# The first unit's decays by other operations, and the pieces of the first two units in one explicit list

## The chip, the cores and the metric

One core of one Trainium2 chip. The time is that of the device from launch to end, in microseconds (us), as the median of several executions. The span in a profile (first to last instruction) is 1.7 to 1.9 us shorter than the time of the same execution, in all executions but two of `tags_old` (2.3 and 2.4).

The five engines work at once, each through its own queue, in order: TensorE (PE, with its weight loads as PEld), VectorE (DVE), ScalarE (ACT), GpSimd (POOL) and SyncE (SP, which here only issues transfers). PSUM is the buffer that TensorE writes its results to. The clock in a profile is the granted clock, the share of TensorE's full clock that it was given in that stretch.

## The reference

A gated linear attention with complex decays, followed by an ELU layer with two weight matrices.

```python
# q, k, v, a_re, a_im: (4, 8, 768, 48) float32
mag   = sqrt(a_re**2 + a_im**2)
scale = minimum(mag, 0.999) / (mag + 1e-6)
for t in range(768):
    S = (a[t] * scale[t]) * S + outer(k[t], v[t])      # complex S, 48 x 48 per head
    y[t] = q[t] @ real(S)
x = y as (3072, 384)
h = x @ w_in                                           # w_in (384, 2048)
g = where(h > 0, h, exp(minimum(h, 0)) - 1)
return (g @ w_out).astype(float32)                     # w_out (2048, 384)
```

The two weight matrices arrive as float64. The kernel makes float32 of them with bit operations on VectorE.

## The kernel before

The work is cut into 12 units of 256 tokens (two batches, 128 positions). For every unit the kernel takes logarithms of the decays' lengths, angles, running sums of both over the positions (by matmuls with a triangular matrix), exponentials and sines; it scales q and k with them, transposes them on TensorE, makes scores, states and values, brings the result into the layer's layout by six small transfers (the "seam"), and then runs the layer: 8 pieces `hidden` (12 matmul instructions each, 2.6 us) and 8 groups `project` (8 instructions each, 2.6 to 2.8 us).

The weights come in 16 parts of 786 KB, 8 of each matrix. Each is converted in five VectorE instructions of 128 x 768, the last of which is the addition below:

```python
    def rounded(kind, m):
        w, dst = raw.pop((kind, m))
        ...
        yield from _rounded(nc, w, f, p)          # four bit operations
        nc.vector.tensor_tensor(out=dst, in0=p, in1=f, op=ALU.add)
        done.append((kind, m))
        yield True

    def converts(n):                              # the next n of these 80 instructions
        ...
```

What comes when is set by numbers. Every piece of work is put into a plan with a position; the plan is sorted, and the result is the order in which each engine's queue is filled:

```python
    decays_of(0, *map(us, (6, 8, 8, 13.4, 13, 13.2, 13.3, 13.5, 13.5)))
    ...
    layer_of(0, 4, 20)
    layer_of(1, 12, 28)
    ...
    for at in range(4, 24):
        put(at + 0.1, converts, 3)
    ...
    for u in range(2, NU):
        if u == 2:
            decays_of(u, 16, 17, 17, 18.4, 19.5, 19.6, 22.7, 19.8, 19.8)
            gates_of(u, 20.4, 21.6, 22.1, 22.4, 22.6)
    ...
    for _, _, do in sorted(plan, key=lambda x: x[:2]):
        do()
```

So in `before` unit 2's decays and gates (positions 16 to 22.6) stand between the conversions (positions up to 23.1) in VectorE's queue. Every unit also sends its decays at the ends of chunks (64 positions each) through a buffer in DRAM and back, to get them transposed.

Of the kernel before, what the change touches and what calls it, by code (L numbers as in the profile page):

```python
# [16 lines left out]
C = 128  # L17
L = 64
# [486 lines left out]
def kernel(  # L505
# [33 lines left out]
    def const(a, name):  # L539
        a = np.ascontiguousarray(a, dtype=np.float32)  # L540
        t = cst.tile(list(a.shape), FP32, name=name)
        nc.scalar.dma_start(out=t, in_=nc.inline_tensor(a, name=name + "_c").ap())
        return t
# [6 lines left out]
    i = np.arange(C)  # L550
    upto = i[:, None] <= i[None, :]
    own = i[:, None] // L == i[None, :] // L

# [4 lines left out]
    off = cst.tile([C, 4], FP32, name="off")  # L558
# [4 lines left out]
    def work(shape):  # L563
        return ps.tile(shape, FP32, tag="w", bufs=3, name="w")
# [40 lines left out]
    def weights_of(kind, m):  # L605

        if kind == "in":
            n = WF * DM // NI
            dst, cols = w_in[:, :, ts(m, n)], ts(m, 2 * n)
            t = sb.tile([C, WF * DM, 2], U32, tag="g" + str(int(m > 1)), bufs=2, name="w64")  # L610
# [72 lines left out]

    def squares(u):
        x = nat[u]
        ar, ai = x["ar"], x["ai"]
        x["m2"], sq = new("n", 6), new("n", 6)
        nc.scalar.activation(out=x["m2"], in_=ar, func=AF.Square)
        nc.scalar.activation(out=sq, in_=ai, func=AF.Square)  # L689
        products(u).tensor_tensor(out=x["m2"], in0=x["m2"], in1=sq, op=ALU.add)  # L690
        x["sq"] = sq

    def logarithms(u):


        x = nat[u]
        lm = x["m2"]
        x["w"], x["e"], x["t"] = new("n", 6), new("n", 6), new("n", 6)
        nc.scalar.activation(out=x["w"], in_=x["ar"], func=AF.Ln)
        nc.scalar.activation(out=lm, in_=lm, func=AF.Ln)  # L700

    def powers(u):
        x = nat[u]
        nc.scalar.activation(out=x["t"], in_=x["w"], func=AF.Exp, scale=-1.0)
        nc.scalar.activation(out=x["e"], in_=x["m2"], func=AF.Exp, scale=-0.5, bias=ln_eps)

    def ratios(u):
        x = nat[u]
        w, t = x["w"], x["t"]
        products(u).tensor_tensor(out=w, in0=x["ar"], in1=t, op=ALU.mult)  # L710
        products(u).tensor_tensor(out=t, in0=x["ai"], in1=t, op=ALU.mult)

    def lengths(u):
        x = nat[u]
        x["l"] = lm = x["m2"]
# [12 lines left out]
    def noted(u):  # L728
# [3 lines left out]
        if u < 2:  # L732
            sq = nat[u]["sq"]
            for n, (x, scale, bias) in enumerate(((sq, 1.0, most_sq), (ar, -1.0, least_re))):
                nc.scalar.activation(
                    out=sq, in_=x, func=AF.Relu, scale=scale, bias=bias,
                    accum_out=off[:, 2 * n + u : 2 * n + u + 1],
                )
            return
        nc.vector.tensor_reduce(  # L740
            out=least[:, u : u + 1], in_=flat(ar), axis=mybir.AxisListType.X, op=ALU.min
        )
        nc.vector.tensor_reduce(
            out=most[:, u : u + 1], in_=flat(ai), axis=mybir.AxisListType.X, op=ALU.max,
            apply_absolute_value=True,
        )
# [3 lines left out]
    def angles(u):  # L750
        x = nat[u]
        x["th"] = new("n", 6)
# [12 lines left out]
    def turns(u):  # L765
        x = nat[u]
        x["z"] = new("n", 6)
        for n in range(NB):
# [11 lines left out]
            )  # L780
        nxt = u + B // NB
        if nxt < NU:
            carry[nxt] = new("carry", 2, [1, NB * HD])
            nc.gpsimd.dma_start(out=carry[nxt], in_=flat(x["z"])[C - 1 : C])  # L784

    def decays(u):
# [3 lines left out]
        for n in range(NB):  # L790
            t = work([C, HD])
            nc.tensor.matmul(  # L792
                t, lhsT=sum_logs, rhs=x["l"][:, n].rearrange("p h d -> p (h d)"),
                start=True, stop=True,
            )
            for key, sign in (("E", 1.0), ("F", -1.0)):
# [3 lines left out]
                )  # L800
        ends = dram.tile([NB, C // L, H, D], FP32, tag="ends", bufs=2, name="ends")
# [6 lines left out]
    def waves(u):  # L808
        x = nat[u]
        x["cs"] = new("cs", 1, [C, NB * H, 2, D])  # L810
        z = x["z"].rearrange("p n h d -> p (n h) d")
        nc.scalar.activation(out=x["cs"][:, :, 1], in_=z, func=AF.Sin, scale=TURN)
        cos = x["cs"][:, :, 0]
        nc.scalar.activation(out=cos, in_=z, func=AF.Abs)
        nc.scalar.activation(out=cos, in_=cos, func=AF.Sin, scale=-TURN, bias=quarter)

    def scaled(u):
        x = nat[u]
        products(u).tensor_tensor(out=x["k"], in0=x["k"], in1=x["F"], op=ALU.mult)
        nc.vector.tensor_tensor(out=x["q"], in0=x["q"], in1=x["E"], op=ALU.mult)  # L820
# [6 lines left out]
    def gated(u):  # L827

        x = nat[u]
        o = {key: new(key + "g", 1, [C, NB, H, 2, D]) for key in ("k", "q")}  # L830
        step = NB if u > 1 else 1
        for n in range(0, NB, step):
            for key in ("q", "k") if u < 2 else ("k", "q"):
                eng = products(u) if key == "k" else nc.vector
                each = x[key][:, n : n + step].rearrange("p n h d -> p (n h) d")
                eng.tensor_tensor(  # L836
                    out=o[key][:, n : n + step].rearrange("p n h i d -> p (n h) i d"),
                    in0=each.unsqueeze(2).to_broadcast([C, step * H, 2, D]),
                    in1=x["cs"][:, n * H : (n + step) * H], op=ALU.mult,
                )  # L840
# [29 lines left out]
    def states(u, n):  # L870
# [8 lines left out]
        gs = [work([2 * D, H, D]) for c in range(last)]  # L879
# [49 lines left out]
    def seam(u):  # L929

        x = nat[u]
        for j in range(2):
            for i in range(NI):
                eng = nc.scalar if u < 2 and j else nc.gpsimd
                eng.dma_start(  # L935
# [4 lines left out]
    def hidden(u, f):  # L940
        x = nat[u]
# [3 lines left out]
        t = ps.tile([C, 2, GT], FP32, tag="mlp", bufs=3, name="mlp")  # L945
        for e in range(2):
            for i in range(NI):
# [3 lines left out]
                )  # L951
# [198 lines left out]
```

## Time and profile before

| | before |
|---|---|
| time, median of 3 | 768.64 us (766.08 to 769.48) |
| span and time of the profiled run | 763.8 and 765.6 us |
| TensorE busy, of the span | 718.8 us, 94% |
| last weight part converted | 158.5 us |
| first layer piece of unit 2 | 203.1 us |
| from there on, TensorE | full |

Two more lines from the view of waits, VectorE's waits from 0 to 160 us (who waited for what, the total in us, how often, the longest):

```profile
DVE wf L39 <- DMA w<-in_moe_w_in_dram: 11.1, 3, 6.4
...
DVE g L955 <- ACT ee L954: 8.8, 3, 5.2
```

VectorE is the bound of the start, and yet stands still 20 us of it in these two groups alone: because input weights were not there, and because it had come, in its own order, to the second half of a layer piece whose first half ScalarE had not finished.

### The profile page before, as it was taken

How to read it: one execution, taken by the hardware profiler on the slowest of the kernel's cores; microseconds unless marked ns; L12 is line 12 of the kernel's file. 1: busy time of each engine (PE TensorE's matmuls, PEld its weight loads, DVE VectorE, ACT ScalarE, POOL GpSimd, SP SyncE). 2: the span in 40 equal slices, each digit the busy share in tenths (PEclk: the TensorE clock that was granted, in tenths of full speed). 3: DMA queues.
4: the chain of work that ended last, by engine and by line, in shares of the span. 5: the costliest groups of instructions: out<-in, count | busy, mean ns of one | idle time of the engine just before them, and what ended most of it. 6: DMA issues, size and time to landing. Idle time of an engine off the chain costs nothing.

```text
span 763.8 us, 13152 instructions
## 1 busy us (share of the span) xinstructions
PE 718.8 (94%) x5502; PEld 537.6 (70%) x5502; DVE 305.6 (40%) x416; ACT 390.2 (51%) x597; POOL 196.7 (26%) x192
## 2 busy tenths in 40 slices
PE   6978787889999999999999999999999999999995
PEld 5756676456686686686786786786786786786773
DVE  3698579933322532532532432432432423320120
ACT  6755237336445646646546546546546546541220
POOL 0101000104614504504404404405405405402000
PEclk9879899899999999999999999999999999999999
DMA  9959716162320810810810810810800900100000
GB/s 175 161 99 188 124 49 186 42 104 46 65 64 1 163 51 2 160 54 2 169 44 3 172 41 7 169 40 12 167 36 14 168 33 18 52 1 17 10 1 26
DMA packets 143885, 56.09 MB, mean 73 GB/s; under 512 B 128920, under 2 KB 133576, under 8 KB 143816
## 3 DMA queue, kind: packets, MB, share of 16 engines
q1 hardware_dynamic: 139392, 53.49, 34.6%
q0 software_dynamic: 3584, 1.27, 1.6%
q8 instruction: 45, 0.74, 0.4%
q10 hardware_dynamic: 840, 0.40, 0.2%
q14 instruction: 24, 0.20, 0.1%
HBM read 49.14 MB, written 4.79 MB: 71 GB/s over the span
## 4 chain that ended last, share of the span: by engine, by line
PE 80%; DVE 6%; DMA 6%; ACT 3%; issue 2%; SPq 1%; POOL 1%; ACTq 0%; DVEq 0%; POOLq 0%
PE mlp L965 30%; PE mlp L948 30%; PE w L853 5%; PE w L882 4%; DMA w<-in_moe_w_in_dram 4%; PE w L861 3%; PE y L912 3%; PE w L792 2%; PE w L770 2%; PE y L905 2%; DMA w<-in_q_dram 1%; DVE wp L49 1%; DVE wf L42 1%; DMA ends<-n 1%; SPq L631 1%
## 5 line engine op out<-in xcount | busy, mean ns | idle before, releaser
L965 PE MATMUL mlp<-w_out,g 128*128 128x384 f32 x768 | 264.8, 494 | 0.2 <-DVE g L955 0.2
L948 PE MATMUL mlp<-x,w_in 128*128 128x256 f32 x1152 | 262.8, 383 | 0.7 <-DMA x<-y 0.7
L948 PEld LDWEIGHTS mlp<-x,w_in 128*128 128x128 f32 x1152 | 216.2, 191 | 33.0 <-ACT o L971 1.3
L965 PEld LDWEIGHTS mlp<-w_out,g 128*128 128x128 f32 x768 | 143.6, 192 | 93.5 <-issue 2.9
L955 DVE SCALAR_TENSOR_TENSOR g<-ee,mlp 128x512 f32<-128x512 f32 x96 | 65.9, 687 | 213.1 <-ACT ee L954 174.7
L953 ACT ACTIVATE ee<-mlp 128x512 f32<-128x512 f32 x96 | 57.2, 596 | 151.1 <-PE mlp L948 150.6
L895 POOL TENSOR_TENSOR S<-S,T 96x384 f32<-96x384 f32 x36 | 35.6, 989 | 218.6 <-DVE S L893 218.6
L954 ACT ACTIVATE ee<-ee 128x512 f32<-128x512 f32 x96 | 60.5, 630 | 2.9
L935 POOL DMA_DIRECT2D x<-y x66 | 32.5, 499 | 59.9 <-ACT y L924 59.8
L971 ACT COPY o<-mlp 128x384 f32<-128x384 f32 x24 | 11.5, 480 | 66.5 <-PE mlp L965 65.6
L893 DVE TENSOR_TENSOR S<-w,S 96x384 f32<-96x384 f32 x40 | 22.1, 552 | 55.3 <-PE w L882 38.1
L920 ACT COPY x<-y 128x384 f32<-128x384 f32 x24 | 11.5, 478 | 62.9 <-PE y L912 62.9
L882 PEld LDWEIGHTS w<-vn,kg 64*96 64x96 f32 x704 | 34.7, 161 | 9.7 <-issue 9.3
L784 POOL DMA_DIRECT2D carry<-n x10 | 5.1, 505 | 130.3 <-DVE n L778 109.7
L882 PE MATMUL w<-vn,kg 64*96 64x48 f32 x704 | 37.8, 247 | 0.0
L853 PE MATMUL w<-ident,qg 128*96 128x128 f32 x192 | 26.5, 284 | 11.9 <-DVE a L866 7.2
L690 POOL TENSOR_TENSOR n<-n 128x768 f32<-128x768 f32 x9 | 16.4, 1819 | 82.9 <-ACT n L689 82.9
L866 DVE TENSOR_TENSOR a<-w,mask 128x512 f32<-128x512 f32 x24 | 16.5, 688 | 51.7 <-PE w L861 51.7
L836 POOL TENSOR_TENSOR kg<-k,cs 128x1536 f32<-128x1536 f32 x9 | 34.1, 3789 | 10.1 <-issue 10.0
L853 PEld LDWEIGHTS w<-ident,qg 128*96 128x96 f32 x192 | 22.4, 131 | 16.0 <-DVE a L866 7.6
L854 ACT COPY qt<-w 96x512 f32<-96x512 f32 x48 | 25.4, 576 | 15.3 <-PE w L853 15.3
L792 PE MATMUL w<-n,sum_logs 128*128 128x384 f32 x48 | 21.8, 585 | 10.0 <-DVE n L716 10.0
(94 smaller groups left out, 784.0 us busy)
## 6 DMA issues: line engine op xcount, KB each, us to landing
w<-in_moe_w_out_dram SPq DMA_DIRECT2D x16, 768.0 KB
w<-in_moe_w_in_dram SPq DMA_DIRECT2D x8, 768.0 KB
w<-in_moe_w_in_dram SPq DMA_DIRECT2D x16, 288.0 KB
vn<-in_v_dram SPq DMA_DIRECT2D x24, 192.0 KB
out_dram<-o SPq DMA_DIRECT2D x24, 192.0 KB
ar<-in_a_re_dram SPq DMA_DIRECT2D x22, 192.0 KB
ai<-in_a_im_dram SPq DMA_DIRECT2D x22, 192.0 KB
q<-in_q_dram SPq DMA_DIRECT2D x22, 192.0 KB
```

Source lines behind the costliest of these rows:

```text
L792: nc.tensor.matmul(t, lhsT=sum_logs, rhs=x["l"][:, n].rearrange("p h d -> p (h d)"), start=True, stop=True,)
L836: eng.tensor_tensor(out=o[key][:, n : n + step].rearrange("p n h i d -> p (n h) i d"), in0=each.unsqueeze(2).to_broadcast([C, step * H, 2, ...
L853: nc.tensor.transpose(t[:, h], x[key + "g"][:, n, h0 + h], ident)
L854: nc.scalar.copy(out=o[:, h0 : h0 + 4], in_=t)
L882: nc.tensor.matmul(g[:, h], lhsT=x["kg"][ts(c, L), n, h], rhs=vn[u % 2][ts(c, L), n, h, 0:D], start=True, stop=True,)
L895: eng.tensor_tensor(out=new_s, in0=new_s, in1=wide, op=ALU.mult)
L935: eng.dma_start(out=x["x"][ds(j * HP + D, G), i], in_=x["y"][ds(j * HP + i * G, G)])
L948: nc.tensor.matmul(t[:, e], lhsT=w_in[:, i, ts(f + e, C)], rhs=x["x"][:, i], start=(i == 0), stop=(i == NI - 1),)
L953: nc.scalar.activation(out=e, in_=t, func=AF.Relu, scale=-1.0)
L954: nc.scalar.activation(out=e, in_=e, func=AF.Exp, scale=-1.0)
L955: nc.vector.scalar_tensor_tensor(out=x["g", f // 8][:, f % 8 : f % 8 + 2], in0=e, scalar=-1.0, in1=t, op0=ALU.add, op1=ALU.max)
L965: nc.tensor.matmul(x["o", n], lhsT=x["g", f // 8][:, f % 8, ts(n, C)], rhs=w_out[:, f], start=(f == 0), stop=(f == NF - 1),)
```

## The change

Two things at once. The first unit's decays use other operations: the squares are joined by TensorE in PSUM (an addition by two accumulating matmuls), VectorE's reciprocal gives the ratio of imaginary to real part, the sum of capped logarithms is split into two accumulating matmuls, and the chunk ends are picked by matmuls instead of a trip through DRAM (units 0 and 1). GpSimd makes the constant matrices instead of four transfers. And the order of the start is an explicit list, up to unit 2's layer; it interleaves the first layers of units 0 and 1 with their attention, moves unit 2's decays behind all conversions, and lets input parts 4 to 7 use the buffers `w64` that the output parts also use. The diff is cut to its main lines.

```diff
-    ident = const(np.eye(C), "ident")
-    sum_turns = const(upto / (2 * np.pi), "sum_turns")
+    ident = const(C, C, "ident")
+    nc.gpsimd.memset(ident, 0.0)
+    nc.gpsimd.affine_select(out=ident, in_=ident, ...)
...
+    def joined(u):                               # u == 0: squares added on TensorE
+        for key in ("m2", "sq"):
+            for n in range(NB):
+                nc.tensor.matmul(x["both"][n], lhsT=ident, rhs=flat(x[key][:, n : n + 1]),
+                    start=(key == "m2"), stop=(key == "sq"))
...
+    def inverses(n):
+        nc.vector.reciprocal(out=x["t"][:, n], in_=x["ar"][:, n])
...
+    def ends(u):                                 # u < 2: picked by matmuls
+                    nc.tensor.matmul(t[:, n, :, h], lhsT=x["E"][:, n, h],
+                        rhs=ident[:, L - 1 :: L], start=True, stop=True)
...
-            t = sb.tile([C, WF * DM, 2], U32, tag="g" + str(int(m > 1)), bufs=2, name="w64")
+            tag = "g" + str(m // 2) if m < 4 else "w64"
...
-    layer_of(0, 4, 20)
-    layer_of(1, 12, 28)
-    for at in range(4, 24):
-        put(at + 0.1, converts, 3)
+    first = [
+        (warm, 3), (warm, 9), (begun, 0), (squares, 0), (fetch, "in", 0), (load_v, 0),
+        ...
+        *3 * [(convert,)], (ends, 1), (inner, 0, 0), (ratios, 1), (scaled, 1), (noted, 1),
+        ...
+        (inner, 1, 12), (inner, 1, 14), (elu, 1, 12), (elu, 1, 14), *15 * [(convert,)],
+        (fetch, "out", 7), *24 * [(convert,)], (project, 1, 0, 0, 4), (project, 1, 0, 4, 8),
+        *10 * [(convert,)], (begun, 2), *5 * [(convert,)], (project, 0, 0, 0, 4),
+        ...
+        (project, 0, 0, 8, 12), (squares, 2), (joined, 2), (logarithms, 2), (noted, 2),
+        ...
+    ]
```

`inner` is the matmul half of a layer piece and `elu` its second half on ScalarE and VectorE.

## The prediction

> **What bounds the kernel now.** I read the page's busy rows and slices first, then the windows, the chain that ended last, and last the timeline of the first 205 us. All times are from the span's start.
>
> The page and its slices:
>
> ```profile
> PE 718.8 (94%) x5502; PEld 537.6 (70%) x5502; DVE 305.6 (40%) x416; ACT 390.2 (51%) x597; POOL 196.7 (26%) x192
> ...
> PE   6978787889999999999999999999999999999995
> ...
> DVE  3698579933322532532532432432432423320120
> ```
>
> A slice is 19 us. TensorE is busy 94% on average, but the loss is all in the first nine slices; there VectorE is the busy engine (9, 9 in slices 7 and 8). The 40% of VectorE is an average over two different kernels: a start and a steady stage. The windows say it with numbers (columns: sum of the stretch, then PE, PEld, DVE, ACT, POOL busy, clock, DMA, GB/s):
>
> ```profile
> 0.00:20.00 20.00, 12.57 (x83) 11.78 (x84) 8.45 (x10) 12.87 (x16) 0.89 (x10) 0.91 1.19 177
> 20.00:40.00 20.00, 18.54 (x231) 15.49 (x232) 13.54 (x20) 16.57 (x24) 2.52 (x3) 0.92 1.17 159
> 40.00:60.00 20.00, 14.99 (x135) 11.47 (x132) 18.44 (x26) 11.18 (x19) 2.79 (x5) 0.74 0.51 99
> ...
> 120.00:140.00 20.00, 15.50 (x49) 10.30 (x49) 18.60 (x25) 12.29 (x16) 0.00 (x0) 0.83 0.62 174
> 140.00:160.00 20.00, 14.14 (x44) 7.98 (x43) 17.63 (x21) 8.34 (x12) 2.64 (x3) 0.91 0.20 31
> ...
> 300.00:400.00 100.00, 100.00 (x750) 75.72 (x750) 36.95 (x50) 53.95 (x84) 36.65 (x34) 1.00 0.39 82
> ```
>
> From 300 us TensorE is never idle: nothing there can be won except by less matmul work, and the change takes none away. The chain says where the steady stage begins:
>
> ```profile
> 152.52 1.75 DVE kg L836
> 154.27 1.68 DVE qg L836
> 156.09 1.63 PE w L853 x8
> ...
> 203.12 8.10 PE mlp L948 x36
> ...
> 260.47 7.77 PE mlp L948 x36
> ```
>
> At 203.12 the first layer of unit 2 (the third of 12) starts; the next unit's starts at 260.47, then every 57.0 us. So the time is (start of that layer) + 560.7 us to the end of the span + 4.8 us between the span of 763.8 and the median of 768.64. I need one number: when the changed kernel reaches that layer. Before it, TensorE has to do two units of 57.0 us, the attention of unit 2 (57.0 less 96 x 0.216 and 64 x 0.322 for the layers = 15.7) and 2.9 of unit 3: 132.6 us. Some 70 of the 203 us are therefore idleness, cold clock and the dummy "warm" matmuls (10.8 + 6.9 + 2.7 = 20.4 us).
>
> What they wait for is weights. They arrive as float64 in 16 parts, each converted by five VectorE instructions:
>
> ```profile
> 50.98 0.56 DVE L39 TENSOR_SCALAR wf<-w 128x768 uint32<-128x768 uint32 x1
> 51.57 0.96 DVE L42 SCALAR_TENSOR_TENSOR wf<-w,wf 128x768 uint32<-128x768 uint32 x1
> 52.56 0.56 DVE L45 TENSOR_SCALAR wp<-wf 128x768 uint32<-128x768 uint32 x1
> 53.16 0.96 DVE L49 SCALAR_TENSOR_TENSOR wp<-w,wp 128x768 f32<-128x768 uint32 x1
> 54.15 0.96 DVE L642 TENSOR_TENSOR w_in<-wp,wf 128x768 f32<-128x768 f32 x1
> ```
>
> From 50.98 to 55.11 that is 4.13 us a part, 66 us for 16. The last part of the output weights is done at 158.5 us, behind unit 2's gates in VectorE's order. So until 158 us the bound is VectorE (118.8 busy of 160 us, summed over the windows) with holes: first data at 5.6 us, 11.1 us waiting for input weights (three waits, by the view of waits), and waits for ScalarE.
>
> **The Trainium skill.**
> "TensorE: Matmul & The Clock Gate", Part 1, says that an idle array falls to half clock and regains it after some 3.4 us of work. The trace agrees: the four matmul instructions of one decay sum took 2.93 us at 18.26 and 1.45 us at 185.39. I count early ones cold.
> "ScalarE: Activation LUTs", What ACT_TABLE_LOAD costs, gives 1283 ns for every switch of set; the trace has 1.28 us each time. The same page's table of sets has one with both exp and ln, but the kernel's loads show that exp after ln costs one here.
> "VectorE: DVE Perf Modes", in its walkthrough's hardware budget, says that reciprocal is an iterative divide with a repeat count of 8. No row of this trace has one. Estimates for 384 elements: 0.56 us if it runs like the trace's other 384-element operations, eight passes at the 0.96 GHz of the skill's opening page 3.2 us.
>
> **The change part by part.**
> (1) Constants made by GpSimd in place of four transfers, the log table loaded ahead of the data: saves the 1.28 us load that followed the data at 5.62, and 0.2 MB of traffic.
> (2) Unit 0's decays. Removed on VectorE: the join of squares 0.96, two ratios shrunk from 1.91 to 1.15, a length from 0.95 to 0.56, a slope 0.95. Added: two reduces 1.9, two reciprocals 1.1 to 6.4, four sign clears (both units) 2.2, small copies 0.6. VectorE ends 2.7 to 8 us of work heavier; the dearer reciprocal would mostly fill the hole from 7 to 12 us in which the first weights are still under way. ScalarE loses an Ln, an Exp and two noted passes with accumulator reads for unit 0 (about 3.9 us) and the Abs of both. Chain of unit 0 as I step it: squares 8.5, joined on TensorE and Ln by 12 (I allow one useless table load), Exp 14.3, sums 16.7, E and F 17.4, arctan 19.5, turns 22.9, gates from 26 to 29.7, against 27.6 to 31.1 before: 1.5 us gained. The picks of the chunk ends (32 matmul instructions by about 0.11, 3.5 us) replace a DRAM round trip of 4.33 + 2 us that ends in a 2.0 us wait of VectorE, but hold VectorE about as long before the scaling.
> (3) Order. First layers of unit 0 and 1 interleaved with attention: unit 0's layer may start near 44 us instead of 57.02. Unit 2's decays move behind all conversions: 15.2 us of VectorE work (0.95 + 3.8 + 0.95 + 2.2 + 1.9 + 3.5 + 1.9) leave the path to the last weight. Input parts 4 to 7 go through the two buffers of unit 1's inputs and then of the output weights, so 12 parts pass through two buffers.
> VectorE to the last conversion, by starts rather than durations: through unit 1's gates with four parts 50.1; part 4 with mask, states and layer 7.1; then 11 parts 45.6, 14 layer pieces at 0.62 8.7, the rest of unit 1's states 2.3. Sum 113.8.
> Holes: 5.5 before data; 4.5 for Ln and the first weights; 4 for the picks; 1.5 in unit 1. That puts the second half of the parts at about 73 us. A part is 786 KB: 4.2 us at the 177 to 188 GB/s of the page's full slices, plus about 2 us from issue to landing. With two buffers and 3.1 us until a buffer is free again, a pair takes about 6.4 + 4.1 = 10.5 us against 8.3 of VectorE; unit 2's inputs (2 MB, 10.5 us) lie in the same queue. Stepped part by part, holes of 6.6 more. Last conversion: 113.8 + 5.5 + 4.5 + 4 + 1.5 + 6.6 = 135.9, say 136 us against 158.5.
> TensorE from there: the last layer piece of unit 1 is at about 118; then 16 projection groups by 2.6 = 41.4 (10 of them need only weights that are there before 130) and 2.9 for unit 2's sums: 162. Unit 2's decays, started at 136, are gated at about 162 too. Then there is no projection left to hide the attention of unit 2: transposes, copies, scores, states on GpSimd (0.82 each), values, six GpSimd issues by 0.5 and 1.6 us landing. I step 23 us for 11.5 of matmuls: 185.
> 185 against 203.1: 18 us earlier. 768.6 - 18 = 750.6; I say 750.
>
> **The rivals.**
> A: Two buffers become the bound. If a pair takes 13 us instead of 10.5 (transfers of input parts took 11.0 and 6.6 us in the chain before, behind other loads), six pairs cost 15 us more; projections after the last weight still need 20.6 + 2.9 us, and some are taken from a queue that was full anyway: net about 10 us, 760. For it: those two rows of the chain (at 68.51 and 85.64). Against: the output parts before were never waited for.
> B: Unit 2's attention, now without projections between, stalls longer, because ScalarE does unit 3's logs and exps between the copies (each switch 1.28) and GpSimd unit 3's products (1.8 to 2.4 each). Another 6 to 10 us: 757 to 760. For it: before, the copies at 178.5 waited until 199.9 for GpSimd to issue the seam.
> C: VectorE runs nearly without holes and transfers keep up: last conversion at 128, the layer at 178: 743.
> D: The steady stage loses something from moved loads. Against: its transfers use 0.39 of the engines; I give it 1 to 2 us at most.
>
> **Range and chances.** A and B each cost up to 10 us and C wins 7; together 741 to 762 for 8 in 10. The 2% line is at 753.3, only 3 us above my number, so faster is 0.62, within 2% 0.35. Slower than 784 would need the start to end later than at 218 us; 0.03.
>
> **What would show it.** The layer of unit 2 should start at 178 to 196 us and later units still follow every 57.0 us; the last conversion at 128 to 144 us; VectorE busy at least 85% from 20 to 130 us; warm matmuls near 9 us; no wait on the DRAM round trip for units 0 and 1; a hole of 8 to 14 us of TensorE between the last projection of unit 1 and the layer of unit 2. I am wrong if unit spacing grows, or if the last conversion is on time and the layer is not (then B), or if VectorE waits for weights over 15 us after 70 us (then A).

## The result, and the profile after

| | before | after |
|---|---|---|
| time, median | 768.12 us (766.08 to 769.48, 4 runs) | 734.42 us (733.75 to 735.36, 4 runs) |
| ratio | | 0.956, 95% interval 0.954 to 0.959 |
| span of the profiled run | 763.8 us | 733.3 us |
| last weight part converted | 158.5 us | 128.5 us |
| last projection group of unit 1 done | 202.4 us | 151.0 us |
| first layer piece of unit 2 | 203.1 us | 173.8 us |
| first layer piece of unit 3 | 260.5 us | 231.6 us |

A ratio is the mean time of one kernel's runs over that of the other's of the same rounds, so it is not quite the ratio of the medians. The changed kernel is 34 us faster, well over the 2% line, and 6.6 us below the low end of my range.

The page of the profile after:

```profile
PE 712.3 (97%) x5496; PEld 531.9 (73%) x5496; DVE 310.6 (42%) x426; ACT 387.3 (53%) x597; POOL 195.8 (27%) x204
...
PE   7989999998999999999999999999999999999996
...
DVE  6889899445324315325325225324323323320120
```

TensorE is at 9 from the fourth slice on but for one, and VectorE's high digits end in the seventh slice instead of the eighth (a slice is 18.3 us here, 19.1 before). VectorE is 5.0 us busier than before (310.6 against 305.6): the operations did not make its work less.

The windows (the sum, then PE, PEld, DVE, ACT, POOL busy, clock, DMA share, GB/s):

```profile
80.00:100.00 20.00, 19.88 (x93) 17.20 (x92) 18.28 (x27) 9.34 (x16) 0.00 (x0) 1.00 0.86 206
100.00:120.00 20.00, 20.00 (x73) 13.42 (x72) 19.45 (x26) 7.66 (x11) 0.00 (x0) 1.00 0.47 158
120.00:140.00 20.00, 20.00 (x64) 11.79 (x63) 15.39 (x19) 6.77 (x8) 0.00 (x0) 1.00 0.33 81
...
160.00:180.00 20.00, 17.52 (x243) 13.65 (x242) 9.24 (x13) 14.66 (x23) 12.58 (x13) 0.97 0.03 8
```

TensorE and VectorE are now both nearly full from 80 us until the weights are done. Where TensorE had 15.50 of 20 us before (120 to 140), it has 20.00. The only hole left lies behind the projections.

The chain that ended last (start, length, what):

```profile
44.75 4.49 PE mlp L1067 x12
...
81.58 25.48 PE mlp L1067 x116
107.06 36.23 PE mlp L1088 x112
...
145.87 5.17 PE mlp L1088 x16
...
175.17 7.14 PE mlp L1067 x32
...
231.57 7.77 PE mlp L1067 x36
```

`mlp L1067` is a first-layer matmul, `mlp L1088` a projection. Unit 0's layer begins at 44.75 us. From 81.58 to 151.04 TensorE does nothing but layers, projections and two sums of unit 2, without a stop. Then comes unit 2's attention alone, and its layer: four instructions at 173.8, and the row at 175.17 once the last two of the six transfers had come. Unit 3's begins at 231.57, and from there a unit takes 57.03 us, as before (260.47 to 659.64 before and 231.57 to 630.75 after: 399.17 and 399.18 us for seven units). The whole gain is made before 174 us: 260.47 - 231.57 = 28.9 us. The two profiled spans differ by 30.5; the other 1.6 us lie after the last matmul, where nothing was changed. And the medians differ by 33.7 because the profiled run of `before` was 2.5 us below its median and that of `after` 0.6 us above.

VectorE's timeline shows the two rows that decide about the prediction:

```profile
96.35 0.56 DVE L39 TENSOR_SCALAR wf<-w 128x768 uint32<-128x768 uint32 x1 [0.44 <-DMA w<-in_moe_w_out_dram]
...
127.53 0.96 DVE L644 TENSOR_TENSOR w_out<-wp,wf 128x768 f32<-128x768 f32 x1
```

The first is the only conversion that waited for output weights, 0.44 us. The second is the last conversion. I had stepped 6.6 us of such waits and an end at 135.9.

### The profile page after: what moved, and what is told of

Same layout as the page of the kernel before. It is cut to its first block, busy times and chain, and to the rows that moved or that the text cites. A ratio compares the mean times of both kernels' runs of the same rounds, so it can differ in the third digit from the quotient of the medians.

```text
span 733.3 us, 13151 instructions
## 1 busy us (share of the span) xinstructions
PE 712.3 (97%) x5496; PEld 531.9 (73%) x5496; DVE 310.6 (42%) x426; ACT 387.3 (53%) x597; POOL 195.8 (27%) x204
## 4 chain that ended last, share of the span: by engine, by line
PE 91%; DVE 3%; ACT 3%; DMA 1%; issue 1%; POOL 0%; SPq 0%; ACTq 0%; DVEq 0%; POOLq 0%
PE mlp L1088 35%; PE mlp L1067 34%; PE w L961 5%; PE w L992 4%; PE w L969 3%; PE y L1022 3%; PE w L825 2%; PE y L1015 2%; PE w L872 2%; DMA ai<-in_a_im_dram 1%; ACT L1057 1%; PE mlp L1163 0%; DVE wf L42 0%; PE mlp L867 0%; POOL x L1047 0%
## 5 line engine op out<-in xcount | busy, mean ns | idle before, releaser
L1067 PE MATMUL mlp<-x,w_in 128*128 128x256 f32 x1152 | 263.2, 383 | 1.7 <-issue 0.8
L1088 PE MATMUL mlp<-w_out,g 128*128 128x384 f32 x768 | 259.9, 490 | 0.0
L1067 PEld LDWEIGHTS mlp<-x,w_in 128*128 128x128 f32 x1152 | 215.6, 191 | 34.5 <-issue 3.0
L1088 PEld LDWEIGHTS mlp<-w_out,g 128*128 128x128 f32 x768 | 142.8, 190 | 93.6 <-DVE w_out L644 0.5
L1078 DVE SCALAR_TENSOR_TENSOR g<-ee,mlp 128x512 f32<-128x512 f32 x96 | 65.9, 687 | 200.0 <-ACT ee L1077 166.5
L1076 ACT ACTIVATE ee<-mlp 128x512 f32<-128x512 f32 x96 | 57.3, 597 | 145.0 <-PE mlp L1067 141.3
L1094 ACT COPY o<-mlp 128x384 f32<-128x384 f32 x24 | 11.5, 479 | 59.9 <-PE mlp L1088 55.8
L1030 ACT COPY x<-y 128x384 f32<-128x384 f32 x24 | 11.5, 478 | 58.1 <-PE y L1022 58.1
L992 PEld LDWEIGHTS w<-vn,kg 64*96 64x96 f32 x640 | 32.4, 164 | 8.5 <-issue 8.1
L944 POOL TENSOR_TENSOR kg<-k,cs 128x1536 f32<-128x1536 f32 x9 | 35.6, 3958 | 10.1 <-issue 10.0
L974 DVE TENSOR_TENSOR a<-w,mask 128x512 f32<-128x512 f32 x24 | 16.5, 687 | 45.4 <-PE w L969 45.4
L992 PE MATMUL w<-vn,kg 64*96 64x48 f32 x640 | 35.3, 250 | 0.1
L969 PEld LDWEIGHTS w<-qt,kt 96*64 96x64 f32 x768 | 25.2, 141 | 10.2 <-ACT n L694 4.4
L969 PE MATMUL w<-qt,kt 96*64 96x64 f32 x768 | 28.5, 229 | 0.9 <-ACT kt L962 0.9
L922 ACT ACTIVATE cs<-n 128x768 f32<-128x768 f32 (+1 forms) x14 | 10.5, 752 | 33.2 <-DVE n L833 33.2
```

What stands on the lines that cost most here:

```text
L944: eng.tensor_tensor(out=o[key][:, n : n + step].rearrange("p n h i d -> p (n h) i d"), in0=each.unsqueeze(2).to_broadcast([C, step * H, 2, ...
L969: nc.tensor.matmul(t[ts(c, L), h], lhsT=x["kt", n][:, h, ts(c, L)], rhs=x["qt", n][:, h, ts(c, L)], start=True, stop=True,)
L992: nc.tensor.matmul(g[:, h], lhsT=x["kg"][ts(c, L), n, h], rhs=vn[u % 2][ts(c, L), n, h, 0:D], start=True, stop=True,)
L1067: nc.tensor.matmul(t[:, e], lhsT=w_in[:, i, ts(f + e, C)], rhs=x["x"][:, i], start=(i == 0), stop=(i == NI - 1),)
L1076: nc.scalar.activation(out=e, in_=t, func=AF.Relu, scale=-1.0)
L1078: nc.vector.scalar_tensor_tensor(out=x["g", f // 8][:, f % 8 : f % 8 + 2], in0=e, scalar=-1.0, in1=t, op0=ALU.add, op1=ALU.max)
```

## The experiments

What I tested, for what I had wrong and for what made the gain:

- **T**: output weights arrive faster than I assumed; the two buffers never bound.
- **P**: interleaving the first layers early lets TensorE finish them early, and what is brought forward is gained in full, since TensorE is the bound from 75 us on.
- **J**: keeping unit 2's decays out of VectorE's queue until the weights are done is worth their own time.
- **O**: the gain is the order's; the new operations are worth little. Its rival is that the operations, which shorten unit 0's chain, make it.
- **W**: the hole of unit 2's attention can be filled. Its rival is that a filled hole reappears as a wait.

Twelve kernels ran. Differences from `after` are worked out as (ratio of the experiment - 0.9564) x 768 us. The interval of a ratio is 3.1 to 4.0 us to either side, that of `after` 2.0, so differences under some 4.5 us are not resolved. The last column is a second reading, from the trace of one execution: when the first layer piece of unit 3 starts. From there to the end the span takes 501.6 to 501.9 us with the new list and 503.3 to 503.6 with the old order, so that the column says where the profiled run stood (231.57 in `after`, 260.47 in `before`).

| run | median us (range) | ratio to before, 95% | against after | unit 3's layer at |
|---|---|---|---|---|
| out_rows | 740.24 (737.11 to 740.53) | 0.964, 0.959 to 0.968 | +5.5 | 237.21 |
| layers_after | 742.73 (740.61 to 746.97) | 0.970, 0.965 to 0.975 | +10.4 | 237.20 |
| decays2_among | 740.00 (739.40 to 744.75) | 0.966, 0.961 to 0.971 | +7.6 | 236.97 |
| ops_old | 736.75 (734.17 to 739.58) | 0.960, 0.955 to 0.965 | +2.7 | 234.78 |
| ops_alone | 767.70 (766.92 to 769.54) | 1.002, 0.997 to 1.006 | +34.7 | 262.81 |
| tags_old | 734.72 (733.44 to 737.47) | 0.959, 0.954 to 0.964 | +1.9 | 231.11 |
| fewer_tables | 732.92 (731.74 to 734.96) | 0.956, 0.951 to 0.960 | -0.7 | 229.84 |
| before_late2 (wrong result) | 787.75 (785.90 to 789.54) | 1.027, 1.022 to 1.031 | | not read |
| before_late3 | 772.48 (772.40 to 773.18) | 1.008, 1.003 to 1.012 | | 267.20 |
| mixed | 763.52 (758.80 to 765.60) | 0.996, 0.992 to 1.001 | +30.7 | 255.46 |
| mixed2 | 742.16 (740.01 to 744.10) | 0.968, 0.963 to 0.973 | +8.9 | 237.08 |
| early_sums | 742.70 (740.76 to 743.95) | 0.969, 0.964 to 0.973 | +9.3 | 238.93 |

One caution about this column: the profiled run of `after` had a low clock in unit 2's attention, after the last projection. The same window in `after` and then in `fewer_tables`, where the projections end within 0.3 us of each other (151.02 and 150.74):

```profile
150.00:160.00 10.00, 8.80 (x86) 7.07 (x85) 4.86 (x5) 8.85 (x13) 4.27 (x4) 0.71 0.61 100
```

```profile
150.00:160.00 10.00, 7.71 (x129) 5.99 (x129) 5.41 (x6) 9.16 (x13) 3.99 (x4) 1.00 0.57 100
```

From the last projection to unit 2's layer `after` took 22.8 us at a mean clock of 0.85. In the profiled runs of `out_rows`, `layers_after`, `decays2_among`, `ops_old`, `tags_old` and `fewer_tables` the same stretch took 21.2 to 21.4 us at 1.00. So the column makes these six look 1.4 to 1.5 us better against `after` than their lists are; for them the end of the last projection is the cleaner mark.

### out_rows: output weights made to arrive as slowly as predicted

```diff
-            pairs = [(t.rearrange("p (f n) two -> p f (n two)", f=WF),
-                moe_w_out[ts(m, WF * C)].rearrange("(f p) n -> p f n", p=C))]
+            words = t.rearrange("p (f n) two -> p f (n two)", f=WF)
+            rows = moe_w_out[ts(m, WF * C)].rearrange("(f p) n -> p f n", p=C)
+            n = 2 * DM // 8
+            pairs = [(words[:, :, ts(j, n)], rows[:, :, ts(j, n)]) for j in range(8)]
```

The same bytes into the same buffers, with rows of 384 bytes in eight transfers a part instead of rows of 3072 bytes in one.

> The changed kernel, with each part of the output weights fetched by eight transfers with rows of 384 bytes instead of one with rows of 3072. Theory T (the term that my prediction mis-sized is the transfer of an output part: I took 4.2 us a part, the slices of the changed kernel's trace reach 356 to 387 GB/s where such parts move, which is near 2.2 us): with slow rows the holes that I predicted come back, the last layer piece of unit 1 moves from 107 us towards 116, and the time from 734.4 to 741 to 747. Rival B (TensorE has a full queue from 75 us on, so slower parts are hidden, and my error lies elsewhere): 734 to 737.

VectorE's timeline in this run, the conversions that waited and the last one:

```profile
92.98 0.56 DVE L39 TENSOR_SCALAR wf<-w 128x768 uint32<-128x768 uint32 x1 [0.97 <-DMA w<-in_moe_w_out_dram]
...
100.72 0.56 DVE L39 TENSOR_SCALAR wf<-w 128x768 uint32<-128x768 uint32 x1 [2.53 <-DMA w<-in_moe_w_out_dram]
...
112.87 0.56 DVE L39 TENSOR_SCALAR wf<-w 128x768 uint32<-128x768 uint32 x1 [1.94 <-DMA w<-in_moe_w_out_dram]
...
134.95 0.96 DVE L644 TENSOR_TENSOR w_out<-wp,wf 128x768 f32<-128x768 f32 x1
```

With a fourth of 1.01 us, the waits for output weights come to 6.4 us, and the last conversion ends at 135.9: the two figures that I had stepped for `after` itself, 6.6 and 135.9. The rates of the two kernels from 60 to 130 us, in 40 slices of 1.75 us, first `after`, then `out_rows`:

```profile
GB/s 0 132 186 131 0 126 222 163 156 105 248 170 129 176 200 359 251 151 222 310 209 242 11 63 378 18 128 321 0 214 235 0 283 167 86 356 12 0 0 0
```

```profile
GB/s 9 0 49 245 152 4 40 258 168 146 128 217 204 132 157 216 201 173 189 208 201 223 199 194 195 9 186 92 119 193 198 112 71 176 178 92 185 193 177 186
```

In the second half only output parts move. There `after` has peaks of 321 to 378 GB/s with idle slices between; with the short rows nothing goes over 223 and the queue is hardly ever idle. So T holds: the step was right and its rate was wrong. The median of 740.24 us lies just under the 741 to 747 that I expected and above the rival's 734 to 737; the last layer piece of unit 1 ended at 111.4, not 116. In the trace the last projection group ends 7.1 us later than in `after` (158.2), and unit 3's layer starts 5.6 us later. Row size and number of transfers were changed together; which of the two slows the transfer is not told apart here.

### layers_after: four layer pieces not brought forward

```diff
-        *3 * [(convert,)], (ends, 1), (inner, 0, 0), (ratios, 1), (scaled, 1), (noted, 1),
+        *3 * [(convert,)], (ends, 1), (ratios, 1), (scaled, 1), (noted, 1),
...
-        (values, 1, 1), (seam, 1), (inner, 0, 8), *3 * [(convert,)], (elu, 0, 6), (elu, 0, 8),
+        (values, 1, 1), (seam, 1), (inner, 0, 0), (inner, 0, 2), (elu, 0, 0), (inner, 0, 4),
+        (elu, 0, 2), (inner, 0, 6), (elu, 0, 4), (inner, 0, 8), *3 * [(convert,)], (elu, 0, 6), (elu, 0, 8),
```

> The changed kernel, with unit 0's first four layer pieces put behind unit 1's attention in TensorE's order instead of between its steps; everything else as it is. Theory P (from 75 us on TensorE is the bound, so 4 pieces of 2.6 us that no longer fit into idle time before 75 us are paid in full): 742 to 746. Rival D (conversions on VectorE set the end, TensorE has slack before 128 us): 734 to 737.

Measured +10.4 us by the ratios, +8.3 by the medians; four pieces of 2.6 us are 10.4. But its runs spread by 6.4 us, and the profiled one, the fastest of them, stands only 5.6 us behind `after`. Its chain:

```profile
72.52 41.64 PE mlp L1067 x192
114.15 36.12 PE mlp L1088 x112
...
180.80 7.14 PE mlp L1067 x32
```

The projections begin at 114.15 instead of 107.06, 7.1 us later, and end 7.0 later: TensorE stays full from 72 us to there, so what it does not do early it does late. The trace shows two thirds of the 10.4 us at that mark, the timed runs all. The slowest of these (746.97 us) is also the one with the lowest mean clock (0.977, the others 0.983 to 0.985). P holds in kind; "in full" is not shown by the trace.

### decays2_among: unit 2's decays among the conversions again

```diff
-        (inner, 1, 12), (inner, 1, 14), (elu, 1, 12), (elu, 1, 14), *15 * [(convert,)],
+        (inner, 1, 12), (inner, 1, 14), (elu, 1, 12), (elu, 1, 14), (begun, 2), (squares, 2), (joined, 2),
+        (logarithms, 2), (powers, 2), *5 * [(convert,)], (lengths, 2), (ratios, 2), (slopes, 2),
+        (angles, 2), *5 * [(convert,)], (carried, 2), (noted, 2), *5 * [(convert,)],
...
-        (project, 0, 0, 8, 12), (squares, 2), (joined, 2), (logarithms, 2), (noted, 2),
+        (project, 0, 0, 8, 12), (begun, 3), (project, 0, 1, 8, 12), (project, 0, 0, 12, 16),
```

> The changed kernel, with unit 2's decays (about 8 us of VectorE work: join, length, ratios, slope, carry, reduces) among the conversions of output parts 4 to 6, as the kernel before had them. Theory J (the last conversions come just in time for the projections, so VectorE work ahead of them delays TensorE): last conversion from 128.5 to 136 or later, TensorE waits there, part is won back because unit 2's attention has its inputs earlier: 736 to 742. Rival N (TensorE has other projections to do, unit 2's attention starts earlier, it gains): 728 to 734.

Measured +7.6 us by the ratios and, in the trace, 6.8 at the last projection and 5.4 at unit 3's layer; the moved VectorE work lasts some 8 us. The last conversion ends at 133.9 instead of 128.5, and the projections wait for it. The same window in both kernels, `after` first:

```profile
128.00:150.00 22.00, 22.00 (x70) 12.94 (x69) 11.74 (x15) 13.72 (x18) 2.03 (x3) 1.00 0.36 82
```

```profile
128.00:150.00 22.00, 17.64 (x49) 10.06 (x50) 5.65 (x7) 2.72 (x4) 0.00 (x0) 0.92 0.39 81
```

TensorE loses 4.4 of 22 us there and part of its clock, although unit 2's decays are done earlier. J holds: the earlier decays bring nothing back, since the projections that follow the last weight are needed anyway.

### ops_old and ops_alone: order without operations, operations without order

`ops_old` keeps the list of `after` and undoes the operations in it: constants by transfer, VectorE and ScalarE decays for unit 0 as in `before`, chunk ends through DRAM, no bit operation for the sines.

```diff
-        if u > 0:
+        if True:                                 # squares joined on VectorE for unit 0 too
             products(u).tensor_tensor(out=x["m2"], in0=x["m2"], in1=x["sq"], op=ALU.add)
...
-        if u < 2:
-            return
+        # every unit writes its chunk ends to DRAM
         ends = dram.tile([NB, C // L, H, D], FP32, tag="ends", bufs=2, name="ends")
...
-        (logarithms, 0), (lengths, 0), (powers, 0), (convert,), (sums,),
+        (logarithms, 0), (powers, 0), (lengths, 0), (convert,),
```

> The changed kernel's list, with all operations of the first two units as before: constants by four (now six) transfers, unit 0's decays with the VectorE join, two powers, slopes, chunk ends through DRAM, Abs on ScalarE. Theory O (the order earns the 33 us; the operations only move where the first 75 us stall): 734 to 740. Rival K (the operations are what makes the early layers possible, without them the chain of unit 0 and 1 is some us longer and all of it arrives at the end): 743 to 752.

Measured +2.7 us, not resolved from zero. In the trace unit 0's first layer piece comes at 49.96 us instead of 44.68, the first projection at 112.16 instead of 107.06, the end of the last at 156.12 instead of 151.02, unit 3's layer at 234.78 instead of 231.57. So 5.1 us are still there when the projections end; most of the shrinking to 3.2 comes from the low clock in the profiled run of `after`.

`ops_alone` is the reverse: the operations of `after` with the positions, loads and buffers of `before`.

```diff
-    first = [ ... ]
+    first = []
+    put(us(6), warm, 40)
+    put(us(6), squares, 0)
+    put(us(6), joined, 0)
+    put(us(8), inverses, 0)
+    ...
+    for at in range(4, 24):
+        put(at + 0.1, converts, 3)
```

> The changed kernel's operations (constants by GpSimd, sums and picks on TensorE, reciprocal, sign clears) in the order of the kernel before, with that kernel's buffers for the input weights. Theory O (operations alone shorten the head of unit 0 by some us, but the weights and VectorE's queue behind it swallow that): 763 to 768. Rival K (they bring a good part of the 33 us): 745 to 758.

Measured 1.002 of `before`: nothing gained. Its last conversion ends at 160.1 us and unit 2's layer begins at 205.0, both a little later than in `before`. So O holds: the order alone makes some 29 to 31 of the 34 us, and the operations are worth about 3 to 5, not resolved by the timed runs, and only within that order. How the order's share divides is shown in part: the two moves taken back singly cost 10.4 and 7.6 us; the rest of the list was not tested piece by piece.

### tags_old and fewer_tables: small parts of the change

```diff
-            tag = "g" + str(m // 2) if m < 4 else "w64"
+            tag = "g" + str(int(m > 1))
```

> The changed kernel with the old buffers for the input weights: parts 2 to 7 through two buffers that become unit 1's layer outputs, instead of parts 4 to 7 through the two that hold unit 1's inputs and then the output weights. Theory O (list and buffers belong together: part 6 then waits for part 4, unit 1's first layer for part 7, but output parts can come early): 735 to 745. Rival F (the buffers are free either way by the time they are needed): 733 to 736.

734.72 us, in rival F's range and just under O's: the other buffers for input parts are worth 2 us by the ratio, not resolved; in the trace the last projection ends 1.0 us later and unit 3's layer starts 0.5 earlier. Since the two buffers `w64` never bind (T), spreading the parts can't earn much.

```diff
-        (table, "exp_and_others"), (joined, 0), (begun, 1), (fetch, "in", 3), (inverses, 0),
+        (joined, 0), (begun, 1), (fetch, "in", 3), (inverses, 0),
...
-        (warm, 10), (table, "exp_and_others"), (convert,), (inner, 0, 4), (waves, 1),
+        (warm, 10), (convert,), (inner, 0, 4), (waves, 1),
```

> The changed kernel without two table loads that are followed at once by another (an exp set ahead of unit 0's logs, another ahead of unit 1's sines): 1.28 us each. If the head of unit 0 arrived at the end, 732 to 733.5; if VectorE's and TensorE's queues swallow it (theory O), 734 to 735.

In `after` two loads of ScalarE tables stand back to back at 9.28 and 10.57 us, 1.28 us each, on unit 0's chain; the first is never used. Without it and another such load the median is 732.92 us, 1.5 below `after`; it is 0.7 by the ratios and 1.7 in the trace. But of the 1.7 only 0.3 is there when the projections end, and unit 0's layer starts no earlier (44.81 against 44.68): the rest is the clock in unit 2's attention, told above. So the trace speaks for O, although the median fell into the other range. It is the best of all versions run, but the difference from `after` is not resolved.

### before_late2 and before_late3: the one move alone, in the old order

If keeping unit 2's decays behind the conversions is worth 7.6 us in the new list, it might be so in the old one. The first try moved only positions:

```diff
-            decays_of(u, 16, 17, 17, 18.4, 19.5, 19.6, 22.7, 19.8, 19.8)
-            gates_of(u, 20.4, 21.6, 22.1, 22.4, 22.6)
+            decays_of(u, 22.5, 23, 23, 23.2, 23.3, 23.4, 25.7, 23.8, 23.8)
+            gates_of(u, 24, 24.6, 25.1, 25.4, 25.6)
...
-        values_of(u, *(max(r + 22, 24.5) + x for x in (0, 1, 2, 3, 5, 4, 5, 6, 7, 8, 9)))
+        values_of(u, *(max(r + 22, 26.5) + x for x in (0, 1, 2, 3, 5, 4, 5, 6, 7, 8, 9)))
```

> The kernel before, with unit 2's decays, gates and attention planned behind the conversions (its slots moved by some 4 to 6), nothing else. Theory L (this one move takes 15 us of VectorE work off the path to the last conversion, and about half of it is gained): last conversion near 145 instead of 158.5 us, time 756 to 763. Rival I (the head is bound by arrival of the weights, whose buffers free late, and only the new list and buffers help): 764 to 769.

The result is wrong (relative error 0.29): with unit 2's attention moved too, a load for unit 4 came ahead of it and overwrote the v of unit 2. Its time says only that the attention slid into the layer: conversions ended at 146.2, but the layer began at 223.8.

The second try keeps the attention where it was, and every load but one: unit 3's decays are loaded 1.3 positions later, which the expectation does not mention.

```diff
-        put(r + 5.5 * (u < 3) + 7 * (u == 3), load_a, u)
+        put(r + 5.5 * (u < 3) + 8.3 * (u == 3), load_a, u)
...
-            decays_of(u, 16, 17, 17, 18.4, 19.5, 19.6, 22.7, 19.8, 19.8)
-            gates_of(u, 20.4, 21.6, 22.1, 22.4, 22.6)
+            decays_of(u, 23.15, 23.2, 23.2, 23.3, 23.3, 23.4, 24.2, 23.45, 23.45)
+            gates_of(u, 23.5, 23.6, 23.7, 23.8, 24)
```

> The kernel before with unit 2's decays and gates planned behind the conversions, its attention and every load where they were (this mends the earlier try, which computed wrongly because unit 4's values overwrote unit 2's). Conversions should end near 146 us instead of 158.5. Theory S (TensorE then waits in its order for unit 2's sums and transposes, so only part arrives): 758 to 768. Rival L (all 12 us arrive): 754 to 758.

It is right, and 6 us slower than `before`, beyond the range I gave. The conversions are done at 142.0 instead of 158.5, yet unit 2's layer begins at 209.8 instead of 203.1. The longest of TensorE's waits from 120 to 210 us tells where it went, with the same wait in `before` (60 to 205 us) behind it:

```profile
PE w L792 <- DVE n L716: 11.6, 1, 11.6
```

```profile
PE w L792 <- DVE n L716: 4.3, 1, 4.3
```

TensorE had the weights for its projections at 142, but in its queue the sums of unit 2 (L792) stood ahead of most of them, and it waited 11.6 us for those: VectorE began the decays only at 142.0. That is 7.3 us more than before. Unit 2's attention then began at 162.8 instead of 156.1, 6.7 us later, and the layer kept that distance. A queue that could run early stops at the next thing that was ordered for the old time. In `after` the projections stand ahead of the sums.

### mixed, mixed2 and early_sums: filling the hole of unit 2's attention

I had reckoned that after the projections TensorE does 11.5 us of unit 2's attention in 23. Three versions tried to win the rest. (The windows of `after` from 151.06 to 173.79 show TensorE busy 19.37 of 22.73 us, at a mean clock of 0.85 and with sums of unit 3 among it: 3.4 us of idleness, or some 5 in the runs at full clock, where the same work was 16.5 us. There was less to win than I thought.)

`mixed` put unit 2's products on GpSimd, its decays among the conversions and its attention among the projections, and left out the useless table loads.

```diff
-        return nc.vector if u < 3 else nc.gpsimd
+        return nc.vector if u < 2 else nc.gpsimd
...
+        (squares, 2), (joined, 2), (logarithms, 2), (powers, 2), *5 * [(convert,)],
+        (lengths, 2), (project, 1, 0, 4, 8), (project, 0, 0, 4, 8), (decays, 2), (ratios, 2),
+        ...
```

> The changed kernel with unit 2's products on GpSimd (idle from 45 to 148 us), its decays during the conversions, one useless table load taken out of the first unit's chain and one of unit 1's, and its attention mixed with the last projections. Theory P (9 us of TensorE idleness between 151 and 175 us are what is left to win, as the attention of unit 2 runs there alone): 724 to 729. Rival J (VectorE's work for unit 2 delays the last conversions as much as is won): 732 to 738.

763.52 us: nearly all of the gain is lost. In this stretch of the timeline VectorE's conversions (L39, L42) run beside two products on GpSimd:

```profile
112.09 2.59 POOL L750 TENSOR_TENSOR n<-ar,n 128x768 f32<-128x768 f32 x1 [3.93 <-ACT n L736]
112.94 2.16 DVE L39 TENSOR_SCALAR wf<-w 128x768 uint32<-128x768 uint32 x1
114.76 2.00 POOL L751 TENSOR_TENSOR n<-ai,n 128x768 f32<-128x768 f32 x1
115.14 2.44 DVE L42 SCALAR_TENSOR_TENSOR wf<-w,wf 128x768 uint32<-128x768 uint32 x1
```

The one takes 0.56 us in this run where GpSimd rests, and the other 0.96. The first began at 112.94, GpSimd's product ended at 114.68, and 114.68 + 0.56 is 115.24, where 115.10 was the end; the second likewise: 116.76 + 0.96 against 117.58. So VectorE did not run slowly, it stood until GpSimd was done. The Trainium skill says this in "SBUF — State Buffer", Who interferes with whom: a VectorE instruction with two SBUF inputs contends with a GpSimd instruction that reads SBUF, `tensor_scalar` can too, and the loser "fully blocks". This run agrees. In the steady stage TensorE is full in spite of GpSimd's products (100.00 of 100 us from 300 us on); beside the conversions VectorE has no time to spare. Besides, ScalarE's copy of an output waited 9.2 us, until 155.8, for the transfer of an earlier one to DRAM, which SyncE issued at 152.3 behind ten loads for unit 3; and the last conversion ended at 141.3. That these two make up the whole loss is not shown.

`mixed2` kept the products on VectorE and the conversions first, and put unit 2's sums before the last projections and its attention between them.

```diff
+        (project, 1, 0, 8, 12), (project, 0, 0, 8, 12), (project, 0, 1, 8, 12),
+        (begun, 2), (squares, 2), (joined, 2), (logarithms, 2), (noted, 2), (powers, 2),
+        (lengths, 2), (project, 1, 0, 12, 16), (decays, 2), (ratios, 2),
+        ...
+        (project, 1, 1, 0, 4), (project, 1, 1, 4, 8), (transposed, 2, "k", 0), (states, 2, 0),
+        (begun, 3), (squares, 3), (project, 1, 1, 8, 12), (transposed, 2, "q", 0),
```

> The changed kernel up to its last layer piece of unit 1, then: projections sorted so that those that need the last weights come late, unit 2's products on VectorE as in the change, its exponentials before its arctan (two table loads less), its attention between the last four projections, unit 3's transposes later; and two useless table loads removed in the head. Theory P (the 9 us of TensorE idleness in unit 2's attention can be won): 724 to 730. Rival W (unit 3's decays follow the attention and make the same hole later): 733 to 738.

742.16 us, slower than `after`. Its attention is done earlier, but right before the layer TensorE waits 4.1 us for unit 3's first sums, at 171.9, and again 1.7 us at 182.7 in the layer for its second: ScalarE and VectorE had not had time for them in the stretch that was filled. The layer of unit 2 starts at 174.6, that of unit 3 5.5 us later than in `after`. The hole moved behind the attention.

`early_sums`, on top of `fewer_tables`, put unit 2's sums two groups earlier and the last projection between the transposes and the scores.

```diff
-        (begun, 3), (project, 0, 1, 8, 12), (project, 0, 0, 12, 16), (powers, 2),
-        (project, 1, 0, 8, 12), (load_a, 3), (ratios, 2), (slopes, 2), (angles, 2),
+        (begun, 3), (project, 0, 1, 8, 12), (project, 1, 0, 8, 12), (project, 0, 0, 12, 16),
+        (powers, 2), (lengths, 2), (project, 0, 1, 12, 16), (decays, 2), (ends, 2), (load_a, 3),
```

> The changed kernel without the two useless table loads, with unit 2's sums two projection groups earlier, its lengths before its ratios, the DRAM round trip of its ends earlier, and the last projection group between its transposes and scores. If the idleness of TensorE from 151 to 174 us can be cut by starting the attention 3 us earlier: 728 to 731. If unit 3's decays on ScalarE set the pace there: 732 to 735.

742.70 us, 10 us slower than `fewer_tables` by the ratios and 9.1 in the trace, with unit 2's layer at 180.8 (172.1 in `fewer_tables`). TensorE's longest waits from 120 to 185 us:

```profile
PE w L961 <- ACT qt L962: 4.1, 1, 4.1
PE w L825 <- DVE n L813: 2.4, 1, 2.4
```

The first is a transpose that waits for ScalarE's copy of the one before, and ScalarE was, from 159.1 to 166.5, at squares, logarithms and exponentials of unit 3 with two table loads between. This is the prediction's rival B, which `after` itself had avoided. Moving a step forward on one engine let another engine's later work come in front of the copy. The wait is only part of the loss: from 160 to 184 us the clock was 0.72, against 1.00 in `fewer_tables`, and after the wait the 32 matmuls of L992 took 2.80 us where `fewer_tables` has 1.56. An idle TensorE cost more here than the length of its wait. Theory W fails in all three: the hole may be fillable, but none of these lists did it, and I leave it open.

## Why the prediction was wrong

It had 750 us and measured was 734.42. The sign and the order of what bounds the start (VectorE's queue, the last weight, TensorE) were right; three terms of the sum were too large. Predicted was 185 (unit 2's layer) + 560.7 (from there to the end) + 4.8 (span to time) = 750.5. Measured: 174.5, which is 231.57 less one unit of 57.03, + 558.8 + 1.1 = 734.4. So the error of 16.1 us is 10.5 + 1.9 + 3.7.

1. **"A part is 786 KB: 4.2 us at the 177 to 188 GB/s of the page's full slices", hence "holes of 6.6 more".** This is the step that failed. It cost 5.5 us of time in `out_rows`, which made the assumption true. I had taken the rate from slices of 19 us. In the first of them the queue is full, but mostly with q, k, v and decays in rows of 192 bytes; in the seventh, three output parts and a unit's v move in bursts of over 400 GB/s with idle time between, and its mean of 186 is the rate of no transfer. I used such means for rows of 3072 bytes. The Trainium skill says in "DMA: Bandwidth & Descriptors", Specifications, that line rate needs transfers of at least 512 bytes; I had not looked there. The profile of `before` had the number as well, in the view of transfers from 100 to 150 us, where six output parts and one unit's v move (slices of 1.25 us, two of its lines):

```profile
GB/s 26 53 0 0 0 0 0 42 246 342 0 52 310 274 13 49 300 280 0 0 61 322 336 198 174 410 78 0 0 66 295 268 0 0 0 5 0 0 0 3
...
w<-in_moe_w_out_dram SPq DMA_DIRECT2D x6, 768.0 KB
```

A pair such as 246 and 342 is nearly a part: 588 x 1.25 = 735 KB in 2.5 us, where I had 4.2 us for a part. With it the step gives no holes, and 135.9 - 6.6 = 129.3, near the measured 128.5. Rival A, two buffers as the bound, falls by the same lines, and the case of rival C ("last conversion at 128") came true, though its layer at 178 was still 3.5 us late.

2. **"The last layer piece of unit 1 is at about 118; then 16 projection groups".** TensorE's part of it ended at 107.06; VectorE's half of the last piece was done at 111.9. I had counted TensorE's work from the end of VectorE's. TensorE goes ahead by the three PSUM buffers of `mlp`, and its groups fill the time while VectorE still converts. The 44.3 us that follow were right (107.06 to 151.04 is 44.0). In `out_rows`, where the weights bound, the last group ends at 158.2, 22.2 us after the last conversion; I had 162. So of the 11 us by which the projections were done earlier than predicted, 7.1 are the weights and about 4 this count; the attention took half a us more than the 23 I said (174.5 - 151.04). With the right weights both limits meet: 128.5 + 22.2 is 150.7, and TensorE ends at 151.04 without a stop. By this reading a still earlier last weight would have earned nothing; no run tried it.

3. **"4.8 us between the span of 763.8 and the median".** The offset of span to time is 1.8 us. The other 3.0 were the profiled run's distance from the median, that is, scatter of `before`, whose executions span 764.5 to 770.1 us in one set of seven. I had carried it over as a constant. The scatter goes with the granted clock: in that set the fastest run has the highest mean clock (0.973) and the slowest the lowest (0.962). The four runs of `after` lie within 1.6 us, at 0.987 to 0.991.

4. **"560.7 us to the end of the span".** Measured 558.8. Unit spacing is the same to 0.01 us; 1.6 of it lie behind the last matmul, where no code was changed.

What was right: the bound before (VectorE's queue up to the last weight) and after (TensorE); the move of unit 2's decays (`decays2_among`, +7.6); unit 0's layer near 44 us (44.7); VectorE 91% busy from 20 to 130 us, of at least 85% foretold; no rival D. The 23 us for unit 2's attention came true by luck: I had 11.5 us of matmuls and as much idleness, a "hole of 8 to 14 us"; TensorE was busy 19.4 us, at a clock of 0.85, and idle 3.4. The layer at 174.5 lies outside the 178 to 196 that I named, and the last conversion at the early end of its range. Rival B did not come in `after`, but did in `early_sums`. What I read for it in `before` was something else: GpSimd stood idle from 192.2 us and issued the seam at 199.9 because the entry ahead of it in its queue waited 7.1 us for VectorE, not because of its products. The operations' share was small, as said: the chain of unit 0 gained little, the picks cost 1.60 us where I said 3.5, and the warm matmuls shrank from 20.4 to 11.7 us, not to 9. The reciprocals, the term I left open between 0.56 and 3.2 us each, lie between:

```profile
L740 DVE RECIPROCAL n<-ar 128x384 f32<-128x384 f32 x2 | 5.0, 2519 | 0.0
```

2.5 us each, at 6.2 to 11.1 us, while VectorE had little else to do: the first conversion stood behind unit 0's lengths, for which VectorE then waited another 1.6 us for ScalarE.

## What to carry to other kernels

Take a transfer's rate from slices in which that very transfer moves, with its own row length, and short enough to hold no idle time, not from the slices that look full. When an engine's queue is rearranged, count the engine that becomes the bound by its own queue and buffers, and go through every other queue for what now stands ahead of the moved work: one move alone made the old order slower, and the same move inside a list that fits it was worth 7.6 us. Before adding the median's distance from a profile to a prediction, split it into launch overhead, which stays, and scatter, which may not. And before reading a microsecond or two from two traces, compare their granted clocks in the stage concerned.

## What the Trainium skill lacked or had wrong

- "VectorE: DVE Perf Modes" gives the repeat count of 8 for reciprocal but no duration; a reciprocal of 128 x 384 float32 took 2.52 us. My estimate of eight passes at 0.96 GHz, 3.2 us, was too long, and one pass, as for a `tensor_scalar` of that size (0.56 us), far too short.
- "DMA: Bandwidth & Descriptors" names 512 bytes as the least for line rate. The runs agree in direction, up to 378 GB/s with rows of 3072 bytes and at most 223 with 384 bytes from 95 to 130 us; its section Why small descriptors are slow works out an overhead of 27% at 256 bytes from one of its two mechanisms, and the loss here is larger at 384. The eight times as many transfers are part of it, so this is no clean measure of the row length.
- No page that I read says that an engine far from full can hold up the end by the order of its queue alone; here the place of one group of sums held TensorE for 11.6 us with projections ready behind it (`before_late3`), and the place of a copy behind unit 3's exponentials held it for 4.1 (`early_sums`).
